# Placing every split, sum and result of the down phases by itself in a sparse-attention and feed-forward kernel

## Chip, core and metric

The kernel runs on one core of one Trainium2 chip. The metric is the device time of one execution in microseconds; the median of several runs is given.

## What is computed

```python
# q, k, v: (8, 8, 576, 64); w_in: (512, 2048); w_out: (2048, 512)
scores = scale * q @ k^T                       # per batch and head
mask_local   = (rel >= 0) & (rel < 32)         # heads 0..3
mask_strided = (rel >= 0) & (pos[None] % 32 == pos[:, None] % 32)   # heads 4..7
attn = softmax(where(mask, scores, -1e9)) @ v
x = attn as (4608 tokens, 512)
h = x @ w_in
g = where(h >= 1, h, where(h <= -1, 0, (h + 1)**2 / 4))
out = g @ w_out                                # float32
```

## The kernel before

**Float32 by two parts.** Every operand of the feed-forward products is split into a rounded high part and the rest (`split`: a cast on ScalarE, L759, then a subtraction on VectorE, L760), and each product is three matmuls, high x high, high x low, low x high.

**Stages.** The 4608 tokens go through TensorE (PE) as three *chunks* of 512 tokens (0, 1, 2) in the ordinary way, and then as three *blocks* of 1024 tokens (0, 1, 2) by a Strassen-Winograd scheme of seven products in place of eight.
- A chunk has 16 steps `f`, one per 128 hidden features: 12 matmuls of `up` (L665), the gate (`bent`, `squared` on ScalarE, `gated` on VectorE), its split (`rounded`, L693 and L696), and two steps later 12 matmuls of `down` (L710). The `h` of `up` lie in two PSUM banks in turn, so `up` of step f waits for the split of step f - 2.
- A block's *up phase* has 56 steps of six matmuls (L806): seven products (1 to 7) for each of eight pairs of feature tiles. The gates of four pairs-of-pairs `k` are gathered in SBUF as `ga[k]`, `gb[k]` (blocks b11, t3, b21, b22).
- Its *down phase* has 28 steps of 12 matmuls (L907): the products in the order 1, 2, 6, 7, 5, 3, 4, four `k` each (`DOWN`). Step n multiplies the split gates `hl[n]`, which lie in three buffers in turn, so a split can begin when the step three before it is done. Products 6, 5 and 4 need sums of gate blocks first: b11 + t3 (L865), b22 - b11 (L860), b21 - b11 (L862), twelve in all, on VectorE. Results: a copy or an addition out of PSUM (L878 to L889) for each product and half d, and four of the seven write outputs by DMA.
- The sums and splits of the next block's inputs (`x_sum`, L756; `x_split`, L759 and L760) also run in down phases.

**Work between.** The attention of batches 2 to 7, the combinations of weights for the blocks (`SUMS`: four steps each, *combine* on GpSimd L307/L309, *round* on ScalarE L312, *rest* on VectorE L316, *ship* by ScalarE's DMA queue) and the writing back of split weights (`SHIP`) are placed between the matmuls by written tables. A time unit is six matmuls: an up step is 1, a down step 2, a chunk's step 4; chunk 1 begins at 0, chunk 2 at 64, block s at 128 + 112 s. `until(t)`, called at fixed points of the matmul program, issues every entry due before t; that order is the order of the instructions on each engine's queue.

Attention's steps are letters with a unit 0 to 3: `s` scores (PE), `m` mask out of PSUM (VectorE), `x` maximum, `a`/`b` subtract it on GpSimd/VectorE, `e` exponential (ScalarE), `q` total, `p`/`k` add epsilon on ScalarE/VectorE, `r`/`w` normalise on GpSimd/VectorE, `t` transpose (VectorE), `j` spread to DRAM and `J` gather (SyncE's DMA), `v`/`V` times values (PE), `h` and `l` copies out of PSUM (ScalarE, VectorE). Scores and values use the same two PSUM banks. `Q` and `F` load. In the text `v2.b3` is step `v2` of batch 3.

**Where the order was set in the down phase.** The split of step n + 2 (`prep(s, n + 2)`), with its sum just ahead of it, and the results of a finished product stand at fixed places, directly ahead of the matmuls of step n:

```python
if n and DOWN[n - 1][0] != m:
    for d in range(2):
        after(DOWN[n - 1][0], d)
prep(s, n + 2)
```

Only the x steps and attention were placed by the tables there.

Of the kernel before, what the change touches and what calls it, by code (L numbers as in the profile page):

```python
# [75 lines left out]

X_WORK = {0: [(103.03, 1), (106.03, 2), (122.41, -7), (123.8, -6), (123.8, 7), (126.73, -5), (127.38, 5), (127.44, 6),
     (128.28, -4), (129.16, 3), (129.21, 4)],
 1: [(205.07, 1), (206.28, 2), (207.03, -7), (208.7, -6), (213.43, 7), (214.81, -4), (215.28, -5), (218.35, 6),
     (218.77, 5), (224.13, 3), (237.21, 4)],  # L80
 2: [(316.65, -7), (317.01, 1), (318.58, -6), (319.18, 2), (321.64, 7), (325.62, -4), (325.64, -5), (330.83, 6),
     (333.72, 5), (336.7, 3), (348.73, 4)]}
SHIP = [[2.64, 5.47, 9.9, 19.19, 11.97, 21.72, 26.64, 29.9, 33.9, 34.97, 40.51, 47.24, 49.62, 48.01, 57.9, 63.22],
 [65.9, 74.24, 64.69, 76.21, 81.97, 85.9, 87.99, 93.9, 97.9, 103.72, 106.71, 110.82, 113.67, 117.9, 121.64, 125.9]]
# [3 lines left out]
def tile_sparse_attention_then_ffn(  # L88
# [764 lines left out]
    def prep(s, n):  # L853
        if n >= len(DOWN):
            return
        m, k = DOWN[n]
        hl[n] = t = slot(HL_AT[n % 3], [P, 2, 2, CH], F32R, f"hl_{s}_{n}")
        b11, t3, b21, b22 = ga[k][:, 0], ga[k][:, 1], gb[k][:, 0], gb[k][:, 1]
        if m == 5:
            nc.vector.tensor_tensor(out=t3, in0=b22, in1=b11, op=ALU.subtract)  # L860
        elif m == 4:
            nc.vector.tensor_tensor(out=b21, in0=b21, in1=b11, op=ALU.subtract)  # L862
        split(t, {1: b11, 6: b11, 5: t3, 7: t3, 3: b22, 2: b21, 4: b21}[m])
        if m == 2:
            nc.vector.tensor_tensor(out=b11, in0=t3, in1=b11, op=ALU.add)  # L865

    def down_block(s, between):
        acc, kept_ = {}, {}
# [4 lines left out]
        def after(m, d):
            nonlocal room
            y, x, z = (acc.get((q, d)) for q in "yxz")
            if m in (1, 6):
                kept_[m, d] = room[:, d + 2 * (m == 6)]
                nc.scalar.copy(kept_[m, d], y)  # L878
            elif m in (4, 5):
                if (m, d) == (4, 0):  # L880
                    room = slot(HL_AT[len(DOWN) % 3], [P, 2, CH], F32, f"last_{s}")
# [221 lines left out]
```

## Time and profile before

| | |
|---|---|
| median of 3 runs | 854.35 us (854.35 to 855.88) |
| profiled execution | 859.13 us, its span 857.3 us |
| granted TensorE clock | 0.99 |
| PE busy | 821.8 us (96%) |
| VectorE busy | 575.5 us (67%) |
| ScalarE busy | 496.1 us (58%) |
| GpSimd busy | 215.5 us (25%) |
| stages by the trace | chunk 1 134 to 248, chunk 2 248 to 351, block 0 351 to 445 (up) and to 532 (down), block 1 to 616 and 699, block 2 to 775 and 853 us |

Matmuls are pipelined: their durations overlap, and the time between two starts, not the duration, is what one costs. An engine's busy share is a mean over stages; a wait counts where TensorE stands still. In a row of the timeline the brackets give the idle time of the engine before the instruction and what ended it. Durations with a `q` behind the engine's name are those of its queue (issuing a DMA).

### The profile page before, as it was taken

To read this page: it belongs to the slowest core of one execution; us is meant where nothing else is said; L and a number is where in the kernel's file an instruction comes from. 1 tells how busy PE (TensorE), PEld (TensorE's weight loads), DVE (VectorE), ACT (ScalarE), POOL (GpSimd) and SP (SyncE) were. 2 spreads that over 40 slices of the span, in tenths; PEclk is the share of its full clock that TensorE was granted. 3 is DMA by queue.
4 is the path that set the end of the run, shared out by engine and by line. 5 is a ranking of instruction groups with operands and counts; after the bars stand their busy time and mean duration, and the time that the engine had idled before them with its cause. 6 is when DMAs were issued, how large, how long until landed. Compare 5 with 4: busy or idle time off the path is not lost.

```text
span 857.3 us, 17861 instructions
## 1 busy us (share of the span) xinstructions
PE 821.8 (96%) x6965; PEld 660.9 (77%) x6965; DVE 575.5 (67%) x857; ACT 496.1 (58%) x864; POOL 215.5 (25%) x221
## 2 busy tenths in 40 slices
PE   8999999969989999899999989999999999999997
PEld 6788887757877888687878867888887778888885
DVE  5899876667546556756677786765578844567574
ACT  5888954435444455566774543767744537785442
POOL 6355344682217354022220000211200001111000
PEclk9999999999999999999999999999999999999999
DMA  9926436777668767988998756887766666666764
GB/s 351 408 87 211 144 112 243 258 261 249 198 224 286 267 226 246 278 261 244 296 298 228 241 177 218 255 258 222 208 202 199 188 219 198 195 195 185 218 214 135
DMA packets 101795, 195.10 MB, mean 228 GB/s; under 512 B 17104, under 2 KB 32464, under 8 KB 99664
## 3 DMA queue, kind: packets, MB, share of 16 engines
q1 hardware_dynamic: 92496, 164.60, 60.8%
q10 hardware_dynamic: 9216, 29.36, 8.8%
q8 instruction: 55, 0.90, 0.4%
q14 instruction: 28, 0.23, 0.1%
HBM read 147.26 MB, written 46.66 MB: 226 GB/s over the span
## 4 chain that ended last, share of the span: by engine, by line
PE 68%; DVE 16%; ACT 8%; DMA 3%; POOL 2%; issue 2%; ACTq 0%; POOLq 0%; DVEq 0%
PE y L806 14%; PE o L710 12%; PE h L665 11%; PE yo L907 8%; PE z L806 7%; DVE hl L760 5%; PE xo L907 4%; ACT hl L759 4%; PE xp L569 3%; PE x L806 3%; PE sc L406 2%; DVE xs L756 1%; DVE ga L860 1%; DVE gb L862 1%; POOL xs L309 1%
## 5 line engine op out<-in xcount | busy, mean ns | idle before, releaser
L665 PE MATMUL h<-xq,w 128*128 128x512 f32 x576 | 140.9, 393 | 6.1 <-DVE gl L696 5.3
L806 PE MATMUL y<-x,wr 128*128 128x512 f32 x576 | 143.1, 393 | 0.1
L907 PE MATMUL yo<-hl,wr 128*128 128x512 f32 x576 | 135.1, 392 | 3.7 <-DVE hl L760 3.6
L710 PE MATMUL o<-gh,w 128*128 128x512 f32 x384 | 132.8, 405 | 0.0
L665 PEld LDWEIGHTS h<-xq,w 128*128 128x128 f32 x576 | 107.5, 188 | 32.0 <-DVE gl L696 7.3
L907 PEld LDWEIGHTS yo<-hl,wr 128*128 128x128 f32 x576 | 107.3, 188 | 29.4 <-DVE hl L760 5.9
L806 PEld LDWEIGHTS y<-x,wr 128*128 128x128 f32 x576 | 107.6, 189 | 23.7 <-ACT gb L841 0.5
L710 PEld LDWEIGHTS o<-gh,w 128*128 128x128 f32 x384 | 73.5, 191 | 17.0
L710 PE MATMUL o<-gl,w 128*128 128x512 f32 x192 | 76.3, 397 | 0.6 <-DVE gl L696 0.6
L806 PE MATMUL z<-x,wr 128*128 128x512 f32 x288 | 74.8, 396 | 1.0 <-ACT gab L841 1.0
L907 PE MATMUL zo<-hl,wr 128*128 128x512 f32 x288 | 69.0, 394 | 5.7 <-DVE hl L760 3.1
L472 POOL TENSOR_TENSOR pr<-pr,st 128x384 f32<-128x384 f32 (+3 forms) x22 | 25.5, 1159 | 182.6 <-DVE st L468 182.3
L907 PEld LDWEIGHTS zo<-hl,wr 128*128 128x128 f32 x288 | 53.4, 188 | 20.7 <-DVE hl L760 5.8
L760 DVE TENSOR_TENSOR hl<-ga,hl 128x1024 fp32r<-128x1024 f32 x36 | 44.9, 1246 | 34.8 <-ACT hl L759 34.6
L759 ACT CAST hl<-ga 128x1024 fp32r<-128x1024 f32 x36 | 38.0, 1056 | 51.7 <-DVE ga L860 27.9
L846 POOL TENSOR_TENSOR ga<-gb,ga 128x1024 f32<-128x1024 f32 x9 | 21.6, 2397 | 174.3 <-DVE ga L675 159.2
L806 PEld LDWEIGHTS z<-x,wr 128*128 128x128 f32 x288 | 54.2, 190 | 12.9 <-ACT gab L841 1.5
L672 ACT ACTIVATE tmp<-tmp 128x512 f32<-128x512 f32 x96 | 60.7, 632 | 3.0
L307 POOL TENSOR_TENSOR xs<-w 128x512 f32<-128x512 f32 x32 | 46.5, 1473 | 57.2 <-DMA ks<-xs 23.1
L675 DVE SCALAR_TENSOR_TENSOR h<-h,u 128x512 f32<-128x512 f32 x47 | 32.6, 693 | 32.8 <-ACT u L672 32.5
L309 POOL TENSOR_TENSOR xs<-xs 128x256 f32<-128x256 f32 x64 | 52.2, 815 | 5.0
L669 ACT ACTIVATE u<-h,half 128x512 f32<-128x512 f32 x48 | 32.9, 684 | 34.1 <-PE h L665 28.3
(118 smaller groups left out, 1308.6 us busy)
## 6 DMA issues: line engine op xcount, KB each, us to landing
wr<-ks SPq DMA_DIRECT2D x192, 256.0 KB, 4.0
wr<-kq SPq DMA_DIRECT2D x144, 256.0 KB, 3.3
ks<-xs ACTq DMA_DIRECT2D x16, 1024.0 KB, 4.7
raw<-in_w SPq DMA_DIRECT2D x30, 512.0 KB, 9.6
kq<-w ACTq DMA_DIRECT2D x48, 256.0 KB, 4.0
qk<-in_qk_s SPq DMA_DIRECT2D x16, 604.0 KB, 6.0
qk<-in_qk_l SPq DMA_DIRECT2D x16, 576.0 KB, 6.5
v<-in_v_l SPq DMA_DIRECT2D x21, 384.0 KB, 4.2
```

The lines of the kernel that those rows point to most:

```text
L307: nc.gpsimd.tensor_tensor(out=b[:, :, f] if i else b[:, f], in0=hi, in1=lo, op=ALU.add)
L309: nc.gpsimd.tensor_tensor(out=st[:, to, HF:], in0=st[:, x, HF:], in1=st[:, y, HF:], op=op)
L569: nc.tensor.matmul(xp[p][j * D:(j + 1) * D, n], loaded[b, local, b0 + n][keys, j], qs, start=True, stop=True)
L665: nc.tensor.matmul(o_ps[c, f], wt[f][:, 0, h, x, e:e + P], xq[c][:, y, cc], start=first and n == 0, stop=last and n == len(todo) - 1)
L669: nc.scalar.activation(u, h, AF.Relu, bias=half, scale=0.5)
L672: nc.scalar.activation(u, u, AF.Square)
L675: nc.vector.scalar_tensor_tensor(out=to, in0=h, scalar=1.0, in1=u, op0=ALU.max, op1=ALU.min)
L710: nc.tensor.matmul(o_ps[c][d], wt[f][:, 1, h, x, e:e + P], gs[y], start=f == 0 and n == 0, stop=f == NF - 1 and n == 2)
L759: nc.scalar.copy(t[:, 0], src)
L760: nc.vector.tensor_tensor(out=t[:, 1], in0=src, in1=t[:, 0].bitcast(F32), op=ALU.subtract)
L806: nc.tensor.matmul(to, w_[:, a, c * P:(c + 1) * P], xc[m][:, b, c], start=m in (1, 2, 5) and c + q == 0, stop=c == 1 and q == 2, skip_grou ...
L907: nc.tensor.matmul(to, w_[jj][:, a, d * P:(d + 1) * P], t[:, b, jj], start=m in (1, 2, 5) and k + jj + q == 0, stop=k == NP // 2 - 1 and j ...
```

## The change

- `prep(s, n)` becomes `prep(s, m, k)`, the split alone; the sums become `g_sum(m, k, engine)`; the results become `result(s, m, d)`, in which the copy of product 5 (`r5`) and the addition to it (`r0`) are two steps. All are called by a new table `G_WORK`, 53 to 54 entries a block, in which `s` is a split, `t` a sum on VectorE, `p` a sum on GpSimd, `r` a result (`s61`: product 6, k 1). Two of the twelve sums of each block go to GpSimd: p63 and p43 in block 0, p63 and p41 in block 1, p63 and p53 in block 2.
- `down_block` keeps the matmuls and the weight fetches; `up_block` no longer issues the first two splits.
- The tables `WORK`, `SUMS`, `X_WORK`, `SHIP` and `GATE` have other times: most entries move by less than a slot, some by one or more. Six attention steps change engine (k1.b2 to p1, b1.b4 to a1, r2.b5 to w2, r1.b6 to w1, b3.b6 to a3, p3.b7 to k3).

```diff
-GATE, ROUNDED, BEFORE_BLOCKS = 2.04, 3.18, 128.01
+GATE, ROUNDED, BEFORE_BLOCKS = 2.1, 3.18, 128.01
...
+G_WORK = {0: [(166.41, 's10'), (170.72, 's11'), (185.76, 's12'), (187.75, 's20'), (187.83, 's13'), (190.4, 's21'),
+     (190.62, 't61'), (190.64, 't60'), (191.9, 'r10'), (191.9, 'r11'), (192.3, 's22'), (193.43, 't62'),
+     (196.43, 's23'), (197.08, 's61'), (197.38, 's60'), (198.16, 'r20'), (198.28, 'r21'), (198.95, 'p63'),
+     (200.86, 's62'), (202.29, 's63'), (203.0, 's70'), (206.86, 's71'), (207.63, 'r60'), (207.68, 'r61'),
+     (207.89, 's72'), (208.48, 't50'), (209.49, 's73'), (211.69, 's50'), (213.19, 't51'), (215.59, 't52'),
+     (215.71, 's51'), (215.91, 's52'), (217.59, 't53'), (219.76, 's53'), (220.69, 's30'), (221.84, 's31'),
+     (222.59, 'r50'), (223.92, 'r51'), (225.11, 'r00'), (225.93, 's32'), (226.23, 'r01'), (226.69, 's33'),
+     (227.94, 't40'), (228.94, 't42'), (229.6, 's40'), (229.68, 't41'), (230.95, 's41'), (231.25, 'p43'),
+     (232.07, 'r30'), (232.2, 'r31'), (232.3, 's42'), (235.88, 's43'), (239.9, 'r40'), (239.9, 'r41')],
...
-            if m == 5 and j in (5, 6):
-                prep(s, j - 5)
...
+    def prep(s, m, k):
+        n = DOWN.index((m, k))
+        hl[n] = t = slot(HL_AT[n % 3], [P, 2, 2, CH], F32R, f"hl_{s}_{n}")
+        split(t, {1: ga[k][:, 0], 6: ga[k][:, 0], 5: ga[k][:, 1], 7: ga[k][:, 1], 3: gb[k][:, 1], 2: gb[k][:, 0], 4: gb[k][:, 0]}[m])
+
+    def g_sum(m, k, eng):
         b11, t3, b21, b22 = ga[k][:, 0], ga[k][:, 1], gb[k][:, 0], gb[k][:, 1]
-        if m == 5:
-            nc.vector.tensor_tensor(out=t3, in0=b22, in1=b11, op=ALU.subtract)
-        elif m == 4:
-            nc.vector.tensor_tensor(out=b21, in0=b21, in1=b11, op=ALU.subtract)
-        split(t, {1: b11, 6: b11, 5: t3, 7: t3, 3: b22, 2: b21, 4: b21}[m])
-        if m == 2:
-            nc.vector.tensor_tensor(out=b11, in0=t3, in1=b11, op=ALU.add)
+        to, x, y, op = {6: (b11, t3, b11, ALU.add), 5: (t3, b22, b11, ALU.subtract), 4: (b21, b21, b11, ALU.subtract)}[m]
+        eng.tensor_tensor(out=to, in0=x, in1=y, op=op)
+
+    def result(s, m, d):
+        tokens = T0 + 2 * CH * s
+        y, x, z = (acc.get((q, d)) for q in "yxz")
...
+        t = rooms_["last"][:, d] if m == 4 else rooms_["kept"][:, d + 2 * (m in (3, 6))]
+        if m in (1, 4, 5, 6):
+            nc.scalar.copy(t, z if m == 5 else y)
+        else:
+            nc.vector.tensor_tensor(out=t, in0={0: y, 2: x, 3: z}[m], in1=t, op=ALU.add)
+        if m in (0, 2, 3, 4):
+            put(d + 2 * (m in (0, 4)), tokens + CH * (m in (0, 3)), t)
...
-            if n and DOWN[n - 1][0] != m:
-                for d in range(2):
-                    after(DOWN[n - 1][0], d)
-            prep(s, n + 2)
...
+        for s, work in G_WORK.items():
+            for t, name in work:
+                m, k = int(name[1]), int(name[2:])
+                do, what = {"s": (prep, (s, m, k)), "r": (result, (s, m, k)),
+                            "t": (g_sum, (m, k, nc.vector)), "p": (g_sum, (m, k, nc.gpsimd))}[name[0]]
+                agenda.append((t, 4, do, what))
```

Of the chunks' entries that the prediction names, in the order in which they are issued ahead of the same point (a slot):

| slot | before | after |
|---|---|---|
| chunk 1, f 1, ahead of the gate | q0, s1, Q2, k0 w0, m1 x1 a1 | sum 12's rest, s1, q0, Q2, m1 x1 a1 (k0 and w0 between gate and split) |
| chunk 1, f 4, ahead of the gate | v0.b2, h0.b2, sum 0 rest, j1.b2, sum 2 round, sum 0 ship | sum 0 ship, v0.b2, sum 3 round, sum 2 combine (sum 0's rest a slot before, h0.b2 and j1.b2 after the gate) |
| chunk 1, f 5 | sum 2 ship ahead of the gate, Q0.b3 ahead of the gate | sum 3 ship ahead of the gate, Q0.b3 after the step |
| chunk 1, f 8, ahead of the gate | sum 5 combine, sum 6 round, sum 6 rest | sum 6 round, sum 5 combine, sum 6 rest |
| chunk 1, f 9, ahead of the gate | sum 5 round, t3.b2, s0.b3, m0.b3, ..., v2.b2 | s0.b3, m0.b3, ..., sum 5 round, t3.b2, v2.b2 |
| chunk 2, f 0 | sum 14 round at the end of chunk 1 | sum 1 round after the gate |
| chunk 2, f 2 | v2.b3, s0.b4 ahead of the gate, h2.b3 last | v2.b3 ahead of the step's first matmul, s0.b4, h2.b3 ahead of the gate |
| chunk 2, f 4 | V1.b3, h1, l1 ahead of the gate's split, h3 behind it | V1.b3, h1, l1, h3 half a step sooner, ahead of the split |
| block 0, up | J0.b5 in slot 2, v0.b5 in slot 6 | J0.b5 in slot 1, v0.b5 in slot 6 |

More of the change, by code (lines that the diff above doesn't have):

```diff
@@ L22 @@
 CLASSIC = 3
-GATE, ROUNDED, BEFORE_BLOCKS = 2.04, 3.18, 128.01
-WORK = {2: [(0, 's0 m0 x0 b0'), (2.67, 'e0'), (5.15, 'q0'), (5.57, 's1'), (6, 'Q2 k0 w0 m1 x1 a1'), (9, 't0 e1'),
[40 rows of a table removed]
-SUMS = [((0, 0), 8.6, 15.07, 16.58, 17.74), ((1, 1), 84.6, 91.54, 92.6, 94.96), ((0, 1), 10.6, 17.05, 18.6, 20.6),
[5 rows of a table removed]
[L77 to L84, printed above, removed]
+GATE, ROUNDED, BEFORE_BLOCKS = 2.1, 3.18, 128.01
+WORK = {2: [(0, 's0 m0 x0'), (0.81, 'b0'), (2.19, 'e0'), (5.57, 's1'), (5.7, 'q0'), (6, 'Q2 m1 x1 a1'), (6.55, 'k0'),
[46 rows of a table added]
+SUMS = [((0, 0), 8.24, 14.24, 15.95, 16.3), ((1, 1), 65.07, 66.14, 68.31, 75.12), ((0, 0), 17.92, 26.64, 27.02, 28.08),
[5 rows of a table added]
+X_WORK = {0: [(98.33, 1), (106.19, 2), (122.58, -7), (123.8, -6), (123.8, 7), (124.51, -5), (127.26, 6), (127.38, 5),
+     (128.5, -4), (129.01, 3), (129.21, 4)],
+ 1: [(205.19, 1), (206.09, 2), (207.03, -7), (209.24, -6), (211.66, 7), (213.73, -5), (215.79, -4), (218.77, 5),
+     (221.61, 6), (228.34, 3), (236.69, 4)],
+ 2: [(313.5, 1), (316.64, -7), (318.79, 7), (320.94, -6), (326.75, 2), (328.62, -4), (331.14, -5), (332.43, 6),
+     (333.72, 5), (336.25, 3), (348.73, 4)]}
+G_WORK = {0: [(166.41, 's10'), (170.72, 's11'), (185.76, 's12'), (187.75, 's20'), (187.83, 's13'), (190.4, 's21'),
[26 rows of a table added]
+SHIP = [[2.64, 5.47, 9.9, 19.19, 11.97, 16.54, 29.02, 30.65, 34.32, 34.97, 40.8, 50.13, 44.29, 51.27, 58.12, 63.22],
+ [67.11, 74.24, 64.69, 76.21, 81.97, 85.9, 91.2, 96.68, 96.81, 103.72, 106.95, 110.82, 113.97, 116.62, 121.64, 125.9]]
 @with_exitstack
@@ L722, in tile_sparse_attention_then_ffn @@
     UP = [(j - late, m) for j in range(NP + 1) for m, late in ((1, 0), (7, 1), (2, 0), (3, 1), (6, 0), (4, 1), (5, 0)) if 0 <= j - late < NP]
-    DOWN = [(m, k) for m in (1, 2, 6, 7, 5, 3, 4) for k in range(NP // 2)]
+    M_ORDER = (1, 2, 6, 7, 5, 3, 4)
+    DOWN = [(m, k) for m in M_ORDER for k in range(NP // 2)]
     seq = [x for _ in range(NSC) for x in [(0, j, m) for j, m in UP] + [(1, 2 * k + jj, m) for m, k in DOWN for jj in range(2)]]
@@ L847, in up_block @@
             between(n)
-            if m == 5 and j in (5, 6):
-                prep(s, j - 5)
     hl = {}
[L853 to L856, printed above, removed]
+    def prep(s, m, k):
+        n = DOWN.index((m, k))
         hl[n] = t = slot(HL_AT[n % 3], [P, 2, 2, CH], F32R, f"hl_{s}_{n}")
+        split(t, {1: ga[k][:, 0], 6: ga[k][:, 0], 5: ga[k][:, 1], 7: ga[k][:, 1], 3: gb[k][:, 1], 2: gb[k][:, 0], 4: gb[k][:, 0]}[m])
+    def g_sum(m, k, eng):
         b11, t3, b21, b22 = ga[k][:, 0], ga[k][:, 1], gb[k][:, 0], gb[k][:, 1]
-        if m == 5:
-            nc.vector.tensor_tensor(out=t3, in0=b22, in1=b11, op=ALU.subtract)
-        elif m == 4:
-            nc.vector.tensor_tensor(out=b21, in0=b21, in1=b11, op=ALU.subtract)
-        split(t, {1: b11, 6: b11, 5: t3, 7: t3, 3: b22, 2: b21, 4: b21}[m])
-        if m == 2:
-            nc.vector.tensor_tensor(out=b11, in0=t3, in1=b11, op=ALU.add)
+        to, x, y, op = {6: (b11, t3, b11, ALU.add), 5: (t3, b22, b11, ALU.subtract), 4: (b21, b21, b11, ALU.subtract)}[m]
+        eng.tensor_tensor(out=to, in0=x, in1=y, op=op)
@@ new lines, in tile_sparse_attention_then_ffn @@
+    acc, rooms_ = {}, {}
+    def result(s, m, d):
+        tokens = T0 + 2 * CH * s
+        y, x, z = (acc.get((q, d)) for q in "yxz")
+        if (m, d) == (1, 0):
+            rooms_["kept"] = slot(X_AT[4], [P, 4, CH], F32, f"kept_{s}")
+        elif (m, d) == (4, 0):
+            rooms_["last"] = slot(HL_AT[len(DOWN) % 3], [P, 2, CH], F32, f"last_{s}")
+        t = rooms_["last"][:, d] if m == 4 else rooms_["kept"][:, d + 2 * (m in (3, 6))]
[5 more added lines that the diff above has]
+            put(d + 2 * (m in (0, 4)), tokens + CH * (m in (0, 3)), t)
@@ L867, in down_block @@
     def down_block(s, between):
-        acc, kept_ = {}, {}
-        room = slot(X_AT[4], [P, 4, CH], F32, f"kept_{s}")
-        tokens = T0 + 2 * CH * s
         home = {"y": ("b0", "b1"), "x": ("b2", "b3"), "z": ("b4", "b5")}
[L873 to L881, printed above, removed]
-                t = room[:, d]
-                nc.scalar.copy(t, y if m == 4 else z)
-                if m == 5:
-                    nc.vector.tensor_tensor(out=t, in0=y, in1=t, op=ALU.add)
-                put(2 + d, tokens + (0 if m == 4 else CH), t)
-            elif m in (2, 3):
-                t = kept_.pop((1 if m == 2 else 6, d))
-                nc.vector.tensor_tensor(out=t, in0=x if m == 2 else z, in1=t, op=ALU.add)
-                put(d, tokens + (0 if m == 2 else CH), t)
@@ L912, in down_block @@
             between(n)
-        for d in range(2):
-            after(4, d)
     FREE = {"s0": "oo", "s1": "aa", "s2": "hh", "s3": "oo", "f0": "oo", "f1": "hh", "f2": "oo", "f3": "oo",
```

114 rows, old and new, of tables (G_WORK, SUMS, WORK) are left out of this document.

## Prediction

> **What bounds it now.** I read the busy time by stage first, then TensorE's own timeline, then VectorE's, ScalarE's and GpSimd's where TensorE stood still. The profiled execution took 859.13 us, 4.78 over the median of 854.35; all sums below are differences, made in this trace and taken off the median. By stage (the down phases of blocks 0, 1 and 2, then chunk 1; columns are the stretch, its length, busy time of PE, PEld, DVE, ACT and POOL, granted clock, DMA):
>
> ```profile
> 445.30:532.30 87.00, 82.56 (x570) 65.51 (x568) 63.71 (x60) 42.67 (x59) 2.65 (x2) 1.00 0.70 215
> 616.20:698.70 82.50, 78.68 (x337) 62.52 (x336) 62.52 (x58) 39.33 (x44) 2.40 (x1) 1.00 0.64 198
> 774.90:853.30 78.40, 77.26 (x337) 62.64 (x335) 50.60 (x47) 33.07 (x38) 2.40 (x1) 1.00 0.63 191
> 134.00:248.00 114.00, 103.61 (x1034) 82.98 (x1034) 75.24 (x128) 50.75 (x92) 55.27 (x55) 0.99 0.69 240
> ```
>
> TensorE is the bound: in phase 1 it is busy 78.68 of 82.50, VectorE, the next, 62.52. So the change is worth what it takes from TensorE's standing still, and the first thing to know is the floor of a down phase. TensorE's timeline (start, length, what, and in brackets the idle time before and what ended it):
>
> ```profile
> 453.54 0.93 PE L569 MATMUL xp<-pT,v 54*64 54x64 f32 x48
> ...
> 468.22 1.57 PE L569 MATMUL xp<-pT,v 64*64 64x32 f32 x88
> ...
> 499.07 0.50 PE L907 MATMUL zo<-hl,wr 128*128 128x512 f32 x1 [1.67 <-ACT hl L759]
> 500.33 3.01 PE L907 MATMUL zo<-hl,wr 128*128 128x512 f32 x12 [0.76 <-DVE hl L760]
> ...
> 531.17 1.17 PE L406 MATMUL sc<-qk 64*32 64x64 f32 x96
> ...
> 627.09 11.04 PE L907 MATMUL xo<-hl,wr 128*128 128x512 f32 x48
> 637.97 22.14 PE L907 MATMUL yo<-hl,wr 128*128 128x512 f32 x96
> ```
>
> 48 matmuls start to start take 637.97 - 627.09 = 10.88 us: 2.72 for a step of 12, and 28 x 2.72 = 76.2 for a phase. Phase 1 took 82.5 (6.3 over), phase 2 took 78.4 (2.2 over). Phase 0 took 87.0, of which its three groups of attention hold 0.93 + 1.57 + 1.17 = 3.7: 7.1 over, of which I leave 0.6 to the restarts behind those groups. Standing still that could go: 6.5 + 6.3 + 2.2 = 15.0 us. The bracketed waits name splits of the gates (`hl`). Why they are late, on VectorE, then ScalarE:
>
> ```profile
> 494.37 2.35 DVE L756 TENSOR_TENSOR xs<-xs 128x1024 f32<-128x1024 f32 x2
> 496.64 1.22 DVE L860 TENSOR_TENSOR ga<-gb,ga 128x1024 f32<-128x1024 f32 x1
> 499.05 1.22 DVE L760 TENSOR_TENSOR hl<-ga,hl 128x1024 fp32r<-128x1024 f32 x1 [1.19 <-ACT hl L759]
> ```
>
> ```profile
> 497.97 1.04 ACT L759 CAST hl<-ga 128x1024 fp32r<-128x1024 f32 x1 [4.77 <-DVE ga L860]
> ```
>
> ```profile
> 476.50:510.20 33.70, 30.55 (x130) 23.67 (x129) 28.48 (x26) 17.93 (x22) 0.00 (x0) 1.00 0.62 188
> ```
>
> The sum of gate blocks (L860) stands directly ahead of its own split and behind two sums of the next block's inputs (L756). Sum, cast (L759) and subtraction (L760) run end to end, 496.64 to 500.27 = 3.6 us, more than a step, while ScalarE idles 4.77 and VectorE 1.19. VectorE is busy 28.48 of 33.70 there, so the work fits; its order does not.
>
> **The change, part by part: down phases.** Each of 28 splits, 12 sums and 14 results a block gets its own place; two sums go to GpSimd (6 in all, 6 x 1.22 = 7.3 us off VectorE). I walked block 0's new order from step 11 on by hand: 1.05 a cast, 1.22 a sum or subtraction (the next one can start 1.14 after, as 494.37 to 496.64 shows for two), step 11 ending at 0 and each step 2.72, a split's buffer free when the step three before it is done, its subtraction needed 0.23 into its own step (one matmul of the 12). VectorE's order about product 5 is: sum t50, x sum 6, split 15, x split 7, split 16, t51, x sum 5, t52, split 17, x sum 4, split 18, t53, x split 5, split 19. Taken one behind the other, t51 ends at 12.2; the cast of split 17 runs 12.3 to 13.3, its subtraction, behind t52, 14.5 to 15.7; step 17 needs it at 16.5. Before, the same sum stood one place ahead of the split and the cast could not begin. Splits 18, 20, 22, 24 have a us or more. The tightest are split 19 (21.5 against 22.0) and split 25 (37.5 against 38.3). Early in block 0, s20 stands before s13 on ScalarE, so s13's subtraction ends where step 3 begins, behind the 0.93 us of v2; s61 stands before s60 (0.5 us late by itself), but V1's 1.57 us on TensorE lie between. Blocks 1 and 2 come out with 0.4 us or more everywhere. So nearly all of it goes; next late are those margins. I take 13.5 of 15.0; the ends are 15.0, and 8 if the margins fail at four places by the 1.67 us of 499.07 (4 x 1.67 = 6.7).
>
> Results: two copies or additions at the end of a product, as many as before; r0 (0.68) now apart from r5, with its output DMA. Behind a waiting output on SyncE's queue stand weight fetches, seven ahead, 3.5 steps or 9.5 us: nothing, by that cover; without it, up to the 0.68 of the addition each. What follows the last product (copies, outputs) is unchanged.
>
> **GpSimd's sums.**
>
> ```profile
> L846 POOL TENSOR_TENSOR ga<-gb,ga x9: 2387/2397/2409, 383.5 to 761.4; 128x1024 f32<-128x1024 f32 x9
> L316 DVE TENSOR_TENSOR xs<-xs x16: 1182/1218/2310, 141.2 to 342.3; 128x1024 fp32r<-128x1024 f32 x16
> ```
>
> 2.40 us each instead of 1.22. GpSimd is free (2.65 busy in phase 0), and each sum's inputs are ready at least two steps, 5.4 us, before its cast: hidden; uncovered, a cast on ScalarE waits out its 2.40, with the results behind it, and the split after it. On GpSimd's queue it stands behind the last unit's normalisation, done a phase before, and ahead of the next batch's. It can also hold VectorE up: L316 took 2310 ns, 1.1 over its median, with GpSimd at work. Ends: 0, and 2.40 x 6 = 14.4. I take 0, because the inputs of p63 and p43 are ready in the part of the phase where VectorE has room (products 1, 2 and 6).
>
> The Trainium skill, "SBUF — State Buffer", section "Who interferes with whom", says that a VectorE operation with two SBUF inputs and a GpSimd one that reads SBUF exclude each other, the second blocked for the whole of the first. The trace agrees (2310 against 1218); by that rule alone the upper end, 14.4, would be the price.
>
> **Chunk 1.** TensorE's, ScalarE's and GpSimd's timelines:
>
> ```profile
> 182.43 3.01 PE L665 MATMUL h<-xq,w 128*128 128x512 f32 x12 [2.34 <-DVE gl L696]
> ...
> 190.50 1.79 PE L569 MATMUL xp<-pT,v 54*64 54x64 f32 x48 [3.96 <-DVE pr L457]
> ```
>
> ```profile
> 177.03 1.05 ACT L312 CAST xs<-xs 128x1024 fp32r<-128x1024 f32 x1 [4.86 <-POOL xs L309]
> ...
> 184.82 1.05 ACT L312 CAST xs<-xs 128x1024 fp32r<-128x1024 f32 x1 [3.17 <-POOL xs L309]
> ```
>
> ```profile
> 178.05 3.50 POOL L307 TENSOR_TENSOR xs<-w 128x512 f32<-128x512 f32 x2 [0.93 <-DMA ks<-xs]
> ```
>
> ```profile
> 192.20:196.20 4.00, 4.00 (x14) 3.21 (x13) 3.44 (x5) 3.20 (x9) 0.00 (x0) 0.69 0.67 182
> ```
>
> Rounding a combination (L312) stands ahead of the gate on ScalarE and waits for GpSimd, which waits for the last sums' DMA. 2.34 + 3.96 are lost, and the granted clock is 0.69 after, 12 matmuls in 4.00 instead of 2.72: 7.6 us. Where the ship stood so far, on VectorE and ScalarE:
>
> ```profile
> 153.00 1.22 DVE L316 TENSOR_TENSOR xs<-xs 128x1024 fp32r<-128x1024 f32 x1
> ```
>
> ```profile
> 155.75 0.33 ACTq L319 DMA_DIRECT2D ks<-xs  x1
> ```
>
> The sums are ready at 154.22 and go out at 155.75, behind h0's copies and the next rounding; in the new order the ship stands ahead of both, 1.5 us sooner, and the following one no longer goes out together with Q0.b3's loads, which I count as 1.5 more. So GpSimd's combinations behind it, and the two waits, come 3 us earlier; but the rounding that waited at 184.82 still stands ahead of its gate, so a wait and a slow clock remain. I take -3. Ends: -7.6, and +3, as k0 and w0 now stand between the gate and the split of the chunk's second block on VectorE (two operations; I count two of 1.22 and a restart).
>
> **Chunk 2.** TensorE's timeline:
>
> ```profile
> 247.83 3.01 PE L665 MATMUL h<-xq,w 128*128 128x512 f32 x12 [1.40 <-DVE gl L696]
> ...
> 252.49 0.30 PE L406 MATMUL sc<-qk 64*32 64x64 f32 x2 [0.79 <-ACT xs L623]
> ...
> 275.10 0.32 PE L406 MATMUL sc<-qk 64*64 64x54 f32 x2 [1.73 <-ACT xs L623]
> ```
> v2.b3 moves ahead of the matmul at 247.83 and fills that 1.40. But s0.b4 needs the banks that h2's copies free, and those stand where they stood; of 1.40 + 0.79 I expect 1.2 to stay, so -1. h3.b3 moves from behind the gate's cast to ahead of it, with V1 half a step earlier: the wait of 1.73 goes, and the slow clock behind it (1.3, as at 192): -3. Ends for both: -4.5 and +2 (V1's gather not landed).
>
> **Up phases.**
>
> ```profile
> 362.83 0.30 PE L569 MATMUL xp<-pT,v 64*64 64x32 f32 x4 [2.13 <-DMA pT<-there]
> ```
>
> ```profile
> PE z L806 <- ACT gab L841: 1.0, 1, 1.0
> ```
>
> J0.b5 is issued one weight fetch sooner (about 0.5), and split 1 leaves ScalarE's crowded end of the phase, which gives most of the 1.0: -1.5 (ends -3, +2). Six attention steps change engine (as k1.b2 to p1): under 1 us each, beside TensorE's work: 0; uncovered, their own time.
>
> Moved loads and ships stay within a slot or two on SyncE's and ScalarE's queues, and their users move along: 0, inside the next term. Elsewhere tables move by a slot or two; places with no wait today can only lose. I set +4 for that, about half of what the region at 182 cost (ends 0, +10).
>
> **Sum:** -13.5 - 3 - 4 - 1.5 + 4 = -18.0. 859.13 - 18 = 841 in such an execution, 854.35 - 18 = **836.4** as a median, 2.1% faster.
>
> **Rivals.**
> A. The chunks give their part back: new waits of 8 to 12 in place of -8.5 + 4. For it: GpSimd's chain is late at 177 and at 184 alike, and VectorE's order is new in every block. Against: the two named waits have plain causes that are moved. 854.35 - 13.5 + 5 = 846.
> B. Slower: in the chunks, a rounding ahead of a gate waits for GpSimd at new places, each as dear as the stretch from 177 to 196 (7.6), and nothing else is won there. Two such places (15.2) just eat what the down and up phases give (13.5 + 1.5 = 15.0); three, 22.8, end at 854.35 - 15.0 + 22.8 = 862. For it: sums and roundings change places in every block. Against: sum1's rounding now stands behind its gate, not ahead of it.
> C. The six sums lock VectorE out on the path: -18 + 14.4 gives 851. For: 2310. Against: no wait for L846 stands before a split today. This is also what the quoted page's rule would give.
> D. The change does not do what it says: splits are late because the casts wait for buffers, not order; only the chunks' -4.5 remain: 850. Against: ScalarE's 4.77 is put down to L860, not to PE.
> E. All terms at their good ends, with +4 for new waits: -15.0 - 7.6 - 4.5 - 3 + 4 = -26: 828.
>
> **How the numbers follow.** Forecast (829 to 842) 0.53, A 0.20, B 0.10, C 0.05, D 0.06, E 0.06. Within 0.2% (1.7 us) is about what a measurement cannot tell from no change. Slower is B without the 0.01 that ends near zero: 0.09. Same is that 0.01 and 0.03 from the upper edges of A, C and D: 0.04. Faster: 0.87. The range reaches from E's 828 to D's 850 and leaves out B, and edges of A, C and E: 0.2.
>
> **What would show it.** Right: the down phases' windows at 77 to 78 us net of attention, no wait on `hl` over 0.8, six GpSimd sums of 2.40, no VectorE operation behind them over 2 us on a split; chunk 1's value step waiting less or sooner, no wait before the scores at 275. Wrong: a split standing behind a sum on GpSimd; a new rounding ahead of a gate with TensorE cold behind it; gathers landing after their value step in chunk 2.

## The result and the profile after

The changed kernel takes **835.08 us** (median of 4 runs, 832.96 to 836.89), the kernel before beside it 855.07 (854.35 to 855.88): ratio 0.9765, 95% interval 0.9739 to 0.9791, 20.0 us less. Forecast were 836.4 us, 18.0 less.

The two profiled executions lie further apart than the medians: before's (859.13) was above all its timed runs, after's (832.96, span 830.8, clock 0.998) was the fastest of its four. So the stages are read below from several traces wherever more than one kernel shares them. One execution, the profiled one of e5, was disturbed (1337 us at a clock of 0.557) and is left out, so e5 has the time of three runs and no stages.

Stage lengths in us, each from a start on TensorE's timeline to the next stage's: a chunk starts here with its second `up` (step f = 1; 6.5 and 7.2 us ahead of the figures in the table of the kernel before), a phase with its first matmul:

| kernel | chunk 1 | chunk 2 | up 0 | down 0 | up 1 | down 1 | up 2 | down 2 |
|---|---|---|---|---|---|---|---|---|
| before | 113.3 | 109.8 | 94.6 | 87.0 | 83.9 | 82.5 | 76.2 | 78.4 |
| after | 110.7 | 105.5 | 89.4 | 82.4 | 85.2 | 76.3 | 76.2 | 76.3 |

The windows of after that answer to those of the prediction (three down phases, chunk 1, chunk 2; the same columns):

```profile
430.80:513.20 82.40, 81.21 (x570) 66.16 (x569) 63.95 (x60) 42.58 (x58) 7.75 (x4) 1.00 0.79 238
598.35:674.65 76.30, 76.30 (x337) 62.99 (x336) 63.89 (x56) 39.43 (x44) 8.06 (x3) 1.00 0.70 213
750.80:827.15 76.35, 76.35 (x337) 62.88 (x335) 51.08 (x45) 33.15 (x37) 8.06 (x3) 1.00 0.66 196
125.15:235.85 110.70, 103.54 (x1082) 83.27 (x1080) 73.16 (x125) 50.34 (x91) 54.41 (x55) 0.98 0.74 258
235.85:341.35 105.50, 103.11 (x1177) 82.54 (x1176) 69.84 (x110) 53.85 (x106) 51.33 (x51) 1.00 0.74 253
```

In phases 1 and 2 TensorE is busy for the whole window, and both are at the floor of 28 x 2.72 = 76.2. VectorE is no less busy than before in phase 1 (63.89 against 62.52), so it is not less work that ended the waits. TensorE's timeline of phase 0 shows no wait for `hl` in brackets any more, only 0.92 + 0.20 at the value step of batch 6:

```profile
443.21 11.04 PE L928 MATMUL xo<-hl,wr 128*128 128x512 f32 x48
454.18 0.90 PE L602 MATMUL xp<-pT,v 64*64 64x32 f32 x48
456.00 0.33 PE L602 MATMUL xp<-pT,v 54*64 54x64 f32 x4 [0.92 <-DMA wr<-ks]
456.53 0.80 PE L602 MATMUL xp<-pT,v 54*64 54x64 f32 x36 [0.20 <-DMA pT<-there]
457.26 22.05 PE L928 MATMUL yo<-hl,wr 128*128 128x512 f32 x96
479.15 16.51 PE L928 MATMUL zo<-hl,wr 128*128 128x512 f32 x72
```

VectorE, then ScalarE, at the start of product 5, where before the sum, cast and subtraction of one split ran end to end:

```profile
476.86 1.22 DVE L895 TENSOR_TENSOR ga<-gb,ga 128x1024 f32<-128x1024 f32 x1
477.99 1.22 DVE L790 TENSOR_TENSOR xs<-xs 128x1024 f32<-128x1024 f32 x1
479.13 1.22 DVE L895 TENSOR_TENSOR ga<-gb,ga 128x1024 f32<-128x1024 f32 x1
480.26 1.22 DVE L794 TENSOR_TENSOR hl<-ga,hl 128x1024 fp32r<-128x1024 f32 x1
481.40 1.22 DVE L790 TENSOR_TENSOR xs<-xs 128x1024 f32<-128x1024 f32 x1
482.53 1.21 DVE L794 TENSOR_TENSOR hl<-ga,hl 128x1024 fp32r<-128x1024 f32 x1
```

```profile
478.18 1.05 ACT L793 CAST hl<-ga 128x1024 fp32r<-128x1024 f32 x1 [3.18 <-DVE ga L895]
480.45 1.05 ACT L793 CAST hl<-ga 128x1024 fp32r<-128x1024 f32 x1 [1.22 <-DVE ga L895]
```

Sum t51 (476.86), cast 478.18, subtraction 480.26 to 481.48; step 17 starts at 479.15 + 2.72 = 481.87. The cast still waits for its sum. What is gone is the wait that counts: the next split's sum (479.13) is done before this split's subtraction, not after it.

The price on GpSimd, then on VectorE (min/median/max in ns, first and last start):

```profile
L895 POOL TENSOR_TENSOR gab<-gab x5: 2388/2393/3259, 440.0 to 788.8; 128x1024 f32<-128x1024 f32 x5
L895 POOL TENSOR_TENSOR gb<-gb,ga x1: 3253/3253/3253, 614.6 to 614.6; 128x1024 f32<-128x1024 f32 x1
```

```profile
L794 DVE TENSOR_TENSOR hl<-ga,hl x36: 1210/1224/2961, 407.3 to 796.7; 128x1024 fp32r<-128x1024 f32 x36
L794 DVE TENSOR_TENSOR hl<-gb,hl x27: 1210/1218/3291, 437.5 to 817.4; 128x1024 fp32r<-128x1024 f32 x27
```

Five subtractions of splits took 2.15 to 3.29 us, each beside one of these sums (two of the six sums took 3.25), and TensorE waited for none of them. The waits that are left in the chunks (TensorE's timeline, chunk 1 and the start of chunk 2):

```profile
133.10 3.02 PE L698 MATMUL h<-xq,w 128*128 128x512 f32 x12 [1.40 <-DVE gl L729]
140.16 3.06 PE L698 MATMUL h<-xq,w 128*128 128x512 f32 x12 [1.31 <-DVE gl L729]
159.27 1.38 PE L439 MATMUL sc<-qk 64*64 64x54 f32 x40 [2.35 <-DVE xq L665]
185.57 2.01 PE L602 MATMUL xp<-pT,v 54*64 54x64 f32 x48 [1.82 <-DVE pr L490]
242.85 3.01 PE L698 MATMUL h<-xq,w 128*128 128x512 f32 x12 [0.54 <-DVE gl L729]
246.71 0.30 PE L439 MATMUL sc<-qk 64*32 64x64 f32 x2 [0.85 <-ACT xs L656]
247.26 1.15 PE L439 MATMUL sc<-qk 64*32 64x64 f32 x94 [0.25 <-ACT xs L656]
```

### The profile page after: what moved, and what is told of

It is laid out like the page before. It is cut to its first block, busy times and chain, and to the rows that moved or that the text cites. A ratio compares the mean times of both kernels' runs of the same rounds, so it can differ in the third digit from the quotient of the medians.

```text
span 830.8 us, 17876 instructions
## 1 busy us (share of the span) xinstructions
PE 809.5 (97%) x6965; PEld 657.0 (79%) x6965; DVE 575.6 (69%) x851; ACT 496.3 (60%) x864; POOL 231.8 (28%) x227
## 4 chain that ended last, share of the span: by engine, by line
PE 86%; DVE 5%; DMA 4%; ACT 2%; issue 1%; SPq 1%; POOL 1%; POOLq 0%; DVEq 0%
PE yo L928 15%; PE y L840 15%; PE o L743 14%; PE h L698 13%; PE zo L928 8%; PE z L840 8%; PE x L840 4%; PE xp L602 4%; PE xo L928 3%; PE sc L439 3%; DMA pT<-there 2%; DMA wr<-kq 1%; DVE xs L349 1%; DMA qk<-in_qk_s 1%; DVE pr L490 1%
## 5 line engine op out<-in xcount | busy, mean ns | idle before, releaser
L928 PE MATMUL yo<-hl,wr 128*128 128x512 f32 x576 | 133.0, 390 | 0.1
L505 POOL TENSOR_TENSOR pr<-pr,st 128x384 f32<-128x384 f32 (+3 forms) x24 | 27.4, 1142 | 153.4 <-DVE st L501 146.3
L928 PE MATMUL zo<-hl,wr 128*128 128x512 f32 x288 | 66.1, 390 | 0.0
```

What stands on the lines that cost most here:

```text
L928: nc.tensor.matmul(to, w_[jj][:, a, d * P:(d + 1) * P], t[:, b, jj], start=m in (1, 2, 5) and k + jj + q == 0, stop=k == NP // 2 - 1 and j ...
```

## Experiments

Every experiment changes the kernel after; "old tables" are before's `GATE`, `WORK`, `SUMS`, `X_WORK` and `SHIP`. A ratio is to the kernel before.

**e1, the six sums on VectorE.**

```diff
-... (198.95, 'p63') ... (231.25, 'p43') ...
+... (198.95, 't63') ... (231.25, 't43') ...      # and the four of blocks 1 and 2
```

> The changed kernel with the six GpSimd sums of gate blocks (p63, p43 and so on) put on VectorE at the same places of the table; nothing else. Theory (order): the down phases gained because each sum now stands ahead of its split with other work between; VectorE has 5 us of room in its fullest stretch, so the two sums of 1.22 a block go in beside TensorE's work: 835 within 2, down phases still at 76.3 a phase in blocks 1 and 2, no wait on hl above 0.3. Rival (engine): the gain came from taking 7.3 us off VectorE; then up to 1.2 a sum comes back on TensorE, 838 to 842, and waits on hl return near products 6 and 4.

833.78 us (831.07 to 837.24), ratio 0.9731 (0.9674 to 0.9789). Down phases 81.75, 76.78, 76.32: 234.9 in sum, after's 235.0. TensorE waits for no `hl`. The order gives the gain; GpSimd's share of it is not to be seen. No subtraction of a split takes over 1.27 us here, where VectorE has the sums.

**e2, all 36 sums on GpSimd.**

```diff
-... (190.62, 't61'), (190.64, 't60') ... (208.48, 't50') ...
+... (190.62, 'p61'), (190.64, 'p60') ... (208.48, 'p50') ...      # all t of all blocks
```

> The changed kernel with all 36 sums of gate blocks on GpSimd at the same places; 30 sums more of 2.40 us there, 36.6 us less on VectorE. Theory (order): each has its inputs a step or more ahead, so most stay beside TensorE's work; only where sums follow one another at 2.40 (t50 to t53, t40 to t42) can a cast be late by 1 to 2 us: 836 to 841. Rival (lock): GpSimd's sums and VectorE's two-SBUF-input subtractions shut each other out; each of 30 sums can hold a subtraction for up to 2.40, and subtractions of 2 to 3.6 us appear ahead of waits on hl: 845 to 865.

870.0 us (868.89 to 870.89), ratio 1.0151 (1.0108 to 1.0194). That is over both ranges that I had named. Down phases 99.93, 90.03, 79.57: 269.5, 34.5 more than after's for 30 more sums. GpSimd, VectorE and TensorE in phase 0:

```profile
490.03 9.99 POOL L895 TENSOR_TENSOR gb<-gb,ga 128x1024 f32<-128x1024 f32 x3
```

```profile
494.41 3.37 DVE L794 TENSOR_TENSOR hl<-ga,hl 128x1024 fp32r<-128x1024 f32 x1
497.70 3.40 DVE L790 TENSOR_TENSOR xs<-xs 128x1024 f32<-128x1024 f32 x1
501.02 3.38 DVE L794 TENSOR_TENSOR hl<-ga,hl 128x1024 fp32r<-128x1024 f32 x1
```

```profile
497.83 4.61 PE L928 MATMUL zo<-hl,wr 128*128 128x512 f32 x12 [3.57 <-DVE hl L794]
```

Three sums take 9.99 (2.40 each when alone), and so do the three VectorE operations, from 494.41 to 504.40 (1.22 each when alone): as if the two engines took turns, each operation waiting out the other's. Rival C's mechanism is real. Six sums are slowed too, but stand where no result is due at once.

**e3, the down phases alone** (old tables with `G_WORK`), and **e4, the tables alone** (new tables, down phases as before).

```diff
-WORK, SUMS, X_WORK, SHIP = after's     # e3: before's, G_WORK kept
-G_WORK and result()                    # e4: before's prep(s, n + 2) and after(m, d)
```

> The down phases' change alone: the code and the table of splits, sums and results of the changed kernel, with the other tables (attention, sums of weights, x steps, ships, gate time) of the kernel before. Theory (parts add up): the down phases lose their 13 us, chunks and up phases stay as before: 842, down phases at 83 with attention, 76.5 and 76.5. Rival (the x steps had to move too): with the x sums and splits at their old places VectorE still reaches the splits late in products 5 and 3; the down phases keep 4 us or more of waits: 846 or more.

> The other half: the tables of attention, weight sums, x steps, ships and gate time of the changed kernel with the down phases' splits, sums and results at their fixed places as before. Theory (parts add up): chunks 7 and up phases 4 faster, down phases as before with 15 us over their floor: 844 to 846. Rival (x steps were placed for the new splits): with fixed splits the moved x sums stand worse, and the down phases take 2 or more us longer than before: 847 to 851.

e3: 841.53 us (840.35 to 844.27), ratio 0.9824 (0.9779 to 0.9869); down phases 81.68, 76.93, 76.32, so 234.9. e4: 849.59 us (846.89 to 856.30), 0.9922 (0.9895 to 0.9949); down phases 86.83, 83.01, 78.34, so 248.2, as before (247.9). Each part works by itself: against the kernel before beside them (856.11) the down phases' order gives 14.6 us, the tables 6.5. TensorE still waits for `hl` twice in e3 (0.87 and 0.30), so the new places of the x steps are worth little. e4 came out over my 844 to 846, by time in the rival's band, but what the rival named (longer down phases) is not there.

**f3, sums directly ahead of their own split** (all twelve on VectorE, splits and results where the new table has them), and **f5, the fixed places of before with the sums of products 5 and 4 one split sooner** (new tables otherwise).

```diff
-(208.48, 't50') ... (211.69, 's50')               # f3
+(211.689, 't50'), (211.69, 's50')
...
-    if m == 5: t3 = b22 - b11                      # f5: in prep(s, n), ahead of split n
-    split(t, ...)
+    split(t, ...)
+    if DOWN[n + 1][0] == 5: t3 = b22 - b11         # of step n + 1, behind split n; 4 likewise
```

> All twelve sums of a block are on VectorE and each stands again directly ahead of its own split; splits and results keep the places of the new tables. My theory (what pays in the down phases is that a sum is done before its cast is issued, so that sum, cast and subtraction no longer run end to end, 1.22 + 1.05 + 1.22 and more behind other work against a step of 2.72): down phases return most of the way to those of before, 84 to 87, 80 to 82.5 and 77 to 78.4 instead of 82.4, 76.3 and 76.3; TensorE waits on hl again, 4 to 10 us in all; time 839 to 846. Rival (the places of the splits and results count, the sums' do not): down phases within 1 us of those after in sum, time 834 to 836.

> The new tables with the splits and results of the down phases at the fixed places of the kernel before, all sums on VectorE; but the sums of products 5 and 4 are issued one split sooner, directly behind the subtraction of the split ahead of theirs. My theory (what pays is that a sum is done before its cast is issued): most of what the written table gives comes back: down phases 236 to 241 in sum instead of 248.2 with the sums ahead of their own splits, time 838 to 843. Rival (every split and result must stand where the table has it; the sums alone give little): down phases 245 to 248, time 846 to 850.

f3: 859.52 us (855.85 to 864.07), ratio 1.0031 (1.0007 to 1.0056); down phases 89.86, 88.41, 80.92, so 259.2. Moving the sums back takes away the whole gain of the change, more than I expected. Before had product 6's sums four steps ahead already; here those are adjacent too. Some of the table's splits also stand up to 1.9 units later than the fixed ones (s43 at 235.88 for 234, s53 at 219.76 for 218), which leaves less time for an adjacent sum; no run separates the two. VectorE and ScalarE of f3:

```profile
481.61 1.22 DVE L871 TENSOR_TENSOR ga<-gb,ga 128x1024 f32<-128x1024 f32 x1
484.02 1.23 DVE L770 TENSOR_TENSOR hl<-ga,hl 128x1024 fp32r<-128x1024 f32 x1 [1.19 <-ACT hl L769]
```

```profile
482.94 1.05 ACT L769 CAST hl<-ga 128x1024 fp32r<-128x1024 f32 x1 [3.64 <-DVE ga L871]
```

That is the pattern quoted of before: 3.6 us end to end, VectorE idle for 1.19. f5: 839.80 us (838.16 to 842.19), 0.9806 (0.9782 to 0.9829); down phases 82.25, 79.61, 77.15, so 239.0 against 248.2 of e4, whose only difference is the place of those eight sums a block. A few lines give 9.2 of the 13.2 us that the written table gives (248.2 - 235.0). VectorE of f5:

```profile
480.03 1.22 DVE L872 TENSOR_TENSOR ga<-gb,ga 128x1024 f32<-128x1024 f32 x1
481.16 1.22 DVE L762 TENSOR_TENSOR xs<-xs 128x1024 f32<-128x1024 f32 x1
482.44 1.23 DVE L766 TENSOR_TENSOR hl<-ga,hl 128x1024 fp32r<-128x1024 f32 x1
```

**e5, a weight shipment of chunk 1 later.**

```diff
-SHIP = [[2.64, 5.47, 9.9, 19.19, 11.97, 16.54, ...
+SHIP = [[2.64, 5.47, 9.9, 19.19, 11.97, 21.72, ...
```

> The changed kernel with one entry put back: the write-back of split weights 5, half 0, at 21.72 as before (behind chunk 1's f 4) instead of 16.54. In the trace of the changed kernel its issue holds ScalarE's queue for 2.71 us at 151.19, so rounding, gate and l0.b2 of f 4 come late and the scores at 159.27 wait 2.4 us for l0.b2. Theory (the issue's hold): that wait shrinks to under 0.8, chunk 1 (start of its second up to that of chunk 2) goes from 110.7 to 108.5 to 109.3 us, 833 in all. Rival (l0.b2's own move from f 4 to f 5): the wait stays at 1.5 or more, chunk 1 within 0.7 of 110.7.

835.16 us (830.31 to 836.13), ratio 0.9733 (0.9695 to 0.9770), the time of after. Without its stages it does not show whether the wait moved, but other traces do. The long issue on ScalarE's queue (2.71 us in after) stands in five kernels with after's tables (after, e2, e7, f3, f5: 2.57 to 2.72) and not in three (e1, e4, e8: 0.44 to 0.45). Without it the scores wait 0.15 in place of 2.25 to 2.37, but the value step behind them waits 4.09 to 4.41 in place of 1.03 to 1.82, as here in e1:

```profile
185.77 2.01 PE L602 MATMUL xp<-pT,v 54*64 54x64 f32 x48 [4.41 <-DVE pr L490]
```

Chunk 1 takes 111.3 to 112.2 us without the long issue and 110.0 to 111.8 with it. The two waits trade places, and my theory falls.

**e7, h3.b3 of chunk 2 behind the gate's cast again; e8, J0.b5 a slot later.**

```diff
-(82.88, 'h1 l1'), (82.94, 'h3')      # e7
+(82.88, 'h1 l1'), (83.19, 'h3')
-(129.95, 'J0')                       # e8
+(130.5, 'J0')
```

> The changed kernel with one entry put back: the copies h3.b3 behind the gate's cast of chunk 2, f 4 (as before) instead of ahead of it. Theory (my term for chunk 2): the scores s2.b4 wait for these copies again, 1.7 us and a slow clock behind it, chunk 2 goes from 105.5 to 108 to 109 us: 838. Rival (V1's earlier place is what counts, the copies now come early enough either way): wait under 0.5, chunk 2 within 0.5 of 105.5.

> The changed kernel with one entry put back: gather J0.b5 in the third slot of block 0's up phase (one weight fetch later on SyncE's queue) instead of the second. Theory (my term for the up phase): v0.b5 waits longer by the issue that is now ahead, 0.4 to 0.9 us, and the clock falls again behind it (1 to 2 us): the stage grows by 1.5 to 2.5. Rival (the landing is set by the traffic of the chunk's outputs and weights, not by the place in the queue): the wait within 0.3 of 1.07 and the stage within 0.7.

e7: 835.96 us (832.62 to 838.80), 0.9768 (0.9742 to 0.9794). Chunk 2 is 106.2 instead of 105.5, and the scores wait for h3's copies again, but only so much:

```profile
266.92 0.91 PE L439 MATMUL sc<-qk 64*64 64x54 f32 x46 [0.16 <-ACT xs L656]
```

My cause of the 3 us falls: h3's own place is worth 0.7 in these two traces. That fits the rival, by which V1's group half a step sooner does it; no run moves that group back alone. e8: 835.51 us (835.29 to 836.78), 0.9755 (0.9737 to 0.9772); up phase 0 is 92.4, where kernels with the new J0 have 89.4 to 93.3, and v0.b5 waits 1.15 + 0.73 us, where after has 0.76 + 0.32, but e6 1.55 + 0.64. That does not tell the two apart.

**e6, the gate's buffers in turn through the chunks.** The gate of step f lies in buffer f % 3 of its chunk, and 16 steps are no multiple of 3: step 0 takes the buffer that step 15 of the chunk before still holds. The weights' ring is re-seated so that it does not meet them.

```diff
-short(n + f % 3, F32R, ...
+short(n + (NF * c + f) % 3, F32R, ...
-RING_AT = (1, 4, 6, 2, 5, 0, 3)
+RING_AT = (0, 3, 6, 1, 4, 2, 5)
```

> The changed kernel with the three gate buffers taken in turn over the chunks ((16 c + f) mod 3 instead of f mod 3, and the ring of weights ordered to fit), so that the first split of chunks 1 and 2 no longer needs the buffer that the last down of the chunk before still reads. Theory: the waits of 1.40 and 0.54 for gl at the second up of chunk 1 and 2 go (131.3 and 242.1 in the changed kernel's trace), and the 1.31 behind the first of them at least in part, since VectorE is no longer held back 5 us: 2 to 3.3 us less, 832. Rival: what stands behind the split in the queues (outputs' copies, k0 and w0) keeps the next gate late: under 1 us gained.

**829.13 us** (828.05 to 830.30), ratio 0.9678 (0.9659 to 0.9696): faster than both kernels (no run has one of its two edits alone). Chunk 1 is 107.1 (110.7 in after), chunk 2 103.5 (105.5). All three waits for `gl` quoted of after are gone. Of waits over 0.2 us both chunks keep these two, and one of 0.63 in the last `down` of chunk 2 (0.62 in after):

```profile
155.98 1.38 PE L439 MATMUL sc<-qk 64*64 64x54 f32 x40 [1.56 <-DVE xq L665]
182.34 1.47 PE L602 MATMUL xp<-pT,v 54*64 54x64 f32 x48 [1.89 <-DVE pr L490]
```

**f1, e6 with four small moves** (the weight shipment as in e5; l0.b2 beside h0.b2; V1, h1, l1, h3 of batch 6 later; split 60 ahead of 61), and **f4, f1 without the shipment's move.**

```diff
-(20.54, 'l0')
+(18.14, 'l0')
-(198.36, 'V1'), (198.81, 'h1 l1'), (199.85, 'h3'), (199.89, 'l3')
+(200.2, 'V1'), (200.3, 'h1 l1'), (200.35, 'h3'), (200.36, 'l3')
-(197.08, 's61'), (197.38, 's60')
+(197.38, 's60'), (197.39, 's61')
-11.97, 16.54,      # f1 only
+11.97, 21.72,
```

> The gate's buffers go round through the chunks without a break (as in the run with 829.1), and four small moves beside it: ship 0,5 back behind chunk 1's sixth step, l0 of batch 2 beside h0, V1, h1, l1 and h3 of batch 6 some 1.9 units later (its gather landed late by up to 1.5 us in the first down phase), split 60 ahead of split 61. My theory (each new wait that is taken away is worth its own length, and no more): the first down phase 1.0 to 1.5 shorter, chunk 1 0 to 1 shorter than 107.1, time 827 to 828.5. Rival (the waits trade places, as the ship's did in chunk 1): stages within 0.6 of those with the gate's turn alone, time 829 to 830.

> The gate's buffers in turn and the small moves of l0, V1, h1, l1, h3 and of split 60, as in the run before, but ship 0,5 keeps its new, earlier place. My theory (the ship's place is what shortens chunk 1: with it late, 2.30 on gl and 4.36 on the value step's weights were waited for; with it early 1.56 on the scores and 1.89): chunk 1 back at 106.5 to 107.5, chunk 2 103.2, first down phase 81.5, time 826.5 to 828.5. Rival (the small moves cost chunk 1 its 3.3, the ship nothing): chunk 1 stays at 110 to 111, time 829 to 831.

f1: 831.03 us (828.18 to 834.56), 0.9704 (0.9660 to 0.9749); chunk 1 110.4, down 0 81.5 (82.1 in e6). f4: 832.83 us (830.95 to 837.82), 0.9740 (0.9701 to 0.9780); chunk 1 111.9. Chunk 1 lost 3.3 to 4.8 against e6 with and without the weight shipment's move, so that shipment is not what matters, and my theory falls again; f4 is over the rival's times too. The only other move in chunk 1 is l0.b2, one step of 1 us. TensorE of f4 shows the two waits of before back (2.34 and 3.96 there):

```profile
178.00 3.06 PE L698 MATMUL h<-xq,w 128*128 128x512 f32 x12 [2.48 <-DVE gl L729]
186.28 2.01 PE L602 MATMUL xp<-pT,v 54*64 54x64 f32 x48 [4.13 <-DVE pr L490]
```

Why, on f4's VectorE, GpSimd and queues:

```profile
153.86 1.01 DVE L665 TENSOR_TENSOR xq<-xp,xq 128x384 fp32r<-128x384 f32 x2
154.79 1.91 DVE L349 TENSOR_TENSOR xs<-xs 128x1024 fp32r<-128x1024 f32 x1
```

```profile
155.75 0.80 SPq L375 DMA_DIRECT2D qk<-in_qk_l  x2
```

```profile
156.73 0.33 ACTq L352 DMA_DIRECT2D ks<-xs  x1
```

```profile
166.62 3.29 POOL L340 TENSOR_TENSOR xs<-w 128x512 f32<-128x512 f32 x2 [6.40 <-DMA ks<-xs]
```

l0 (L665) now stands ahead of the rest of a combination (L349), so that combination's ship goes out at 156.73, *behind* the loads of batch 3 (Q0.b3, 155.75). The landing times of that one ship (issues, KB, median us from issue to landing), first of before, then e6, then f4:

```profile
ks<-xs ACTq DMA_DIRECT2D x1, 1024.0 KB, 9.1
```

```profile
ks<-xs ACTq DMA_DIRECT2D x1, 1024.0 KB, 4.9
```

```profile
ks<-xs ACTq DMA_DIRECT2D x1, 1024.0 KB, 9.8
```

In e6 the order is the other way (ship 154.90, loads 157.04). Over all thirteen traces that show the stages, before's and after's among them, that ship lands after 4.0 to 6.2 us where it goes out ahead of those loads (after, e1, e2, e4, e6, e7, e8, f3, f5) and after 9.1 to 9.8 where it goes out behind them (before, e3, f1, f4). Chunk 1 follows: 110.0 to 112.2 against 113.3 and 115.4 with the old gate buffers, 107.1 against 110.4 and 111.9 with the new ones. So does the wait for `gl` ahead of the value step: 1.47 to 2.48 us in the four kernels where the ship goes out behind (before 2.34, e3 1.47, f1 2.30, f4 2.48), none in the nine others.

## Why the prediction was right

| term | predicted | measured | from |
|---|---|---|---|
| down phases | -13.5 | -12.9 | 247.9 to 235.0; e3 234.9 |
| six sums on GpSimd | 0 | 0 | e1 |
| chunk 1 | -3 | -3.1 | mean of before and e3 114.4; of after, e1, e2, e4, e7, e8, f3, f5 111.3 |
| chunk 2 | -4 | -3.5 | 108.9 and 105.4, the same without e7 |
| up phases | -1.5 | -1.6 | up 0, the same kernels: 93.0 and 91.4 |
| new waits | +4 | +0.9 | up 1, the same: 83.9 and 84.8 |
| sum | -18.0 | -20.2 | medians: -20.0 |

*Down phases: mechanism and size right*, and shown by taking it away (f3), by leaving the other tables out (e3) and by giving the earlier sums alone to e4 (f5). The predicted floor is reached in phases 1 and 2. Phase 0 is 82.4 - 3.7 = 78.7 net of attention, a little over the 77 to 78 named; nearly half of the 2.5 over the floor is V1.b6 (0.92 + 0.20), whose gather landed from 455.48 to 456.48, which I had not listed. The hand-walked margins hold: split 17's subtraction ends 0.6 us before it is needed (481.48 against 481.87 + 0.23; predicted 15.7 against 16.5).

*GpSimd's sums: cost right, reason half right.* They are hidden, as said. But "no VectorE operation over 2 us on a split" fell: five took 2.15 to 3.29. A VectorE operation of 1.22 held up for the whole of a GpSimd sum of 2.40 would take 3.6, and 3.37 to 3.40 were seen in the rows of e2. By the Trainium skill, "SBUF — State Buffer", section "Who interferes with whom", a VectorE operation with two SBUF inputs and a GpSimd one that reads SBUF exclude each other, and the second is blocked for the whole of the first. With 3.37 to 3.40 against 3.6, e2 agrees to within 0.25 us. The price is paid only where the blocked operation is due at once: in e2 34.5 us for 30 sums, in after nothing that shows for six.

*Chunk 1: size right, in part by luck; of the two causes named, the second carries it.* The prediction gave 1.5 to the first ship going out sooner and 1.5 to the next one "no longer together with Q0.b3's loads". The first ship does go out 2.6 us sooner in the stage (25.7 us after its start for 28.3), but takes 6.48 us to land for 4.37, so it lands only 0.5 sooner. The next one has landed 36.9 to 37.2 us after the stage's start in all eight kernels with after's tables and old gate buffers, and 42.3 and 43.0 in before and e3. That this order alone is worth the whole 3 is not shown: f1 and f4 turn it round, but beside the other gate buffers. The value step waits sooner in the stage rather than less (e1, e4 and e8 have 4.09 to 4.41 there, before 3.96); what is gone is the wait of 2.34 ahead of it. My later theories, of a weight shipment (e5, f1), were wrong, and f4 showed it. The end that I named against the change, k0 and w0 between gate and split, came as the wait of 1.31 at 140.16 (0.15 at that step before). I had put it at nothing in the -3; the -3.1 is net of it. e6, which leaves k0 and w0 there, has no such wait, so it takes the gate's buffers as well.

*Chunk 2: size right, cause in part wrong.* The wait at 275 went, as said, but of the two moves that I named for it h3's gives 0.7 (e7), and V1's earlier group has no run of its own. v2.b3 did what was said: 1.40 + 0.79 + 0.25 became 0.54 + 0.85 + 0.25, 0.8 less for the 1 predicted, with the scores still waiting for h2's copies.

*Up phases:* the size fits the means, but up 0 alone varies between 89.4 and 93.3 in kernels that have the same tables there; e8 could not show that J0.b5 is the cause. That stays open.

*The term furthest off is the reserve.* I set +4 for tables that move everywhere; +0.9 came in the one stage that no other term covers, up phase 1, in after at two places:

```profile
559.48 1.63 PE L840 MATMUL y<-x,wr 128*128 128x512 f32 x6 [0.48 <-DMA wr<-kq]
561.68 0.92 PE L602 MATMUL xp<-pT,v 54*64 54x64 f32 x44 [0.27 <-DMA pT<-there]
```

That is 3.1 less, more than the 2.2 between forecast and sum. But new waits stand inside other rows too: 1.16 more at 140.16 in chunk 1, and 0.92 + 0.20 in phase 0. With them about 3 of the 4 came (the 2.35 ahead of the scores, which trades places with the value step's wait, not counted), and those two stages won that much more than their rows say. So the reserve was nearly right as a sum of waits, and the rows cannot tell how much of the difference is luck. Of the rivals, C's lock exists but not on the path; A and B did not come, as the new waits stayed at about 3 us; D is excluded by f3 and f5; E's good ends were not reached in chunk 1. A's 846 does not follow from its own terms: -13.5 and -8.5 with 8 to 12 of new waits give 840 to 844.

## What to carry to other kernels

Where an operand needs sum, cast and subtraction on two engines in turn, issue the sum one operand ahead: that alone gave 9.2 of 13.2 us here, with no table. An engine with idle time can take work off a busier one only where the other engine's next result is not due within the lock's length: 6 sums cost nothing that shows, 30 more cost 34.5 us. When a chain through DRAM bounds a stage, look at the order in which its transfer and the bulk loads are issued on all queues: one 1-us copy ahead of a 1 MB ship moved it behind two loads and doubled its landing time, and that stage was 3.3 and 4.8 us longer in the two traces.

## What the runs showed of the hardware that I had not expected

GpSimd and VectorE slow each other both ways: GpSimd's 128x1024 float32 sum grew from 2.40 to 3.25 to 3.4 us, and VectorE's 1.22 to 3.4. TensorE's clock fell behind some waits of about two us already: in e6 the value step's wait of 1.89 is followed by a granted clock of 0.61, in f4 4.13 by 0.50. Not behind all: after's wait of 2.35 ahead of the scores at 159.27 left it at 1.00. What decides is not shown. The windows of four us behind those steps, of e6, f4, then after (the counts take in matmuls that reach over a window's edge):

```profile
183.80:187.80 4.00, 4.00 (x12) 3.18 (x12) 2.54 (x5) 2.53 (x6) 0.31 (x1) 0.61 0.55 166
```

```profile
188.20:192.20 4.00, 4.00 (x11) 3.14 (x10) 3.94 (x7) 2.56 (x7) 0.00 (x0) 0.50 0.53 124
```

```profile
160.60:164.60 4.00, 4.00 (x19) 3.29 (x19) 3.85 (x9) 0.00 (x0) 3.77 (x5) 1.00 0.97 310
```

So a wait can cost more than its own length: behind the 1.89 of e6 the 12 matmuls of `down` take 4.32 us (183.74 to 188.06) where a step of 12 takes 2.72.
